# Wider output matmuls for three of four row blocks: 512 columns per row tile, and the last 128 columns transposed for 512 rows at once

## Chip, cores and metric

One core of a Trainium2 chip. The metric is the device time of one execution in microseconds (us). Every result below is the median of several executions, except where it says "one look" (a single execution), next to executions of the kernel before on the same chip.

## The reference, cut to what matters

```python
xn = layernorm(x)                                   # x: 2048 rows x 640
q  = xn @ wq                                        # 32 heads of 192
s  = softmax(q @ k.T * 192**-0.5) @ v @ wo          # the last 512 keys of the cache
g  = silu((silu(xn @ w_gate) * (xn @ w_up)) @ w_down)
out = x + s * g                                     # 2048 x 640, bf16
```

The kernel works on 4 blocks of 512 rows (0 to 3) and on 16 pairs of heads. "Block pass" is one block for one pair of heads.

## The kernel before

After the feed-forward part come 16 pairs. For each pair: query and score matmuls of four blocks, then the attention-times-V matmuls of four blocks, woven with the output matmuls (`wo`) of the block pass two back. Nearly all of this runs on half of the array's rows: `lo` is rows 0 to 63, `hi` is rows 64 to 127. The two halves work on different products at the same time and write to different PSUM banks. PSUM is the memory that TensorE adds its products up in; VectorE or ScalarE has to read a PSUM tile out before the program may use it again.

```python
def ffn_down(b, u):                     # 8 units a block, 12 matmuls of 320 columns each
    ti, n = divmod(u, 2)
    ...
    for f in range(NF):
        nc.tensor.matmul(dn[:, 0:HD], hTs[b][:, f, ti * P : (ti + 1) * P], wd_sb[:, f, cols], ...)
    nc.scalar.activation(g2[:, t, cols], dn[:, 0:HD], ACT.Silu)

def wo_turn(st, i, qt, turn):           # a row tile: 2 x 320 columns; the halves change banks between turns
    for j in range(3):
        for k, r in enumerate((lo, hi)):
            n = k ^ turn
            m = nc.tensor.matmul(ps[:, n, 0:HD], OTs[i][r, 3 * qt + j, :], wo[r, j, n * HD : (n + 1) * HD], ...)
            after(m, st)                # turn 1 waits for a small GpSimd memset that follows turn 0
    ...

def woven(i):                           # a, b: the two halves of attention; w, x, y, z: four row tiles
    (a, b), (w, x, y, z) = (pv(i, 0), pv(i, 1)), (wo_tile(i - 2, qt) for qt in range(4))
    for part in (*a[:2], drop, w[0], *b[:2], w[1], x[0], *a[2:], x[1], y[0], *b[2:], y[1], z[0]):
        part()
    held.append(z[1])                   # runs where the next pass says drop
```

`x[0]` and `x[1]` are the two turns of one unit. A unit holds one of two `sc` PSUM tiles until VectorE has added it to the sum in SBUF. `a` and `b` hold one of two `mm` tiles each until VectorE has made reciprocals and ScalarE has copied the quotients out.

The softmax here doesn't subtract the row's maximum and nothing guards it: scores larger than these inputs give would overflow.

Of the kernel before, what the change touches and what calls it, by code (L numbers as in the profile page):

```python
# [15 lines left out]
def kernel(  # L16
# [34 lines left out]
    HD = D // 2  # L51
    scale = float(Dh) ** -0.5
# [29 lines left out]
    g2 = res.tile([P, T, D], bf, name="g2")  # L82
# [83 lines left out]
    with ExitStack() as fctx:  # L166
# [125 lines left out]

        def ffn_down(b, u):
            ti, n = divmod(u, 2)
            t = b * 4 + ti
            cols = slice(n * HD, (n + 1) * HD)
            dn = mm_tile()[:, 0, :]
            for f in range(NF):
                nc.tensor.matmul(  # L299
                    dn[:, 0:HD], hTs[b][:, f, ti * P : (ti + 1) * P], wd_sb[:, f, cols],  # L300
                    start=(f == 0), stop=(f == NF - 1),
                )
            nc.scalar.activation(g2[:, t, cols], dn[:, 0:HD], ACT.Silu)

# [66 lines left out]
        for b in range(NB):  # L371
# [4 lines left out]
            for f in range(NF):  # L376
# [9 lines left out]
                if nx and f in (6, 7):  # L386
                    for t in range(4 * b + 2 * f - 8, 4 * b + 2 * f - 6):
                        ln_apply(t)
                        ln_transpose_dma(t)

                if b >= 1 and f % 3:
                    ffn_down(b - 1, u)
                    u += 1
# [27 lines left out]
    sacc = sapool.tile([P, T, D], f32, name="sacc")  # L421
# [4 lines left out]
    Ps, OTs, Obs, xrs = {}, {}, {}, {}  # L426
# [111 lines left out]
    def load_xr(t):  # L538
        xrs[t] = finp.tile([P, D], bf, name="x_r", bufs=8)
        nc.sync.dma_start(out=xrs[t][:], in_=x2[t * P : (t + 1) * P, :])  # L540


# [9 lines left out]

    HALVES = [slice(n * HD, (n + 1) * HD) for n in range(2)]

# [16 lines left out]
    def wo_turn(st, i, qt, turn):  # L571
        ps = st["sc"]
        for j in range(3):
            for k, r in enumerate((lo, hi)):
                n = k ^ turn
                m = nc.tensor.matmul(  # L576
                    ps[:, n, 0:HD], OTs[i][r, 3 * qt + j, :], pairs[i // NB]["wo"][r, j, n * HD : (n + 1) * HD],
                    start=(turn == 0 and j == 0), stop=(turn == 1 and j == 2), skip_group_check=True,
                )
                after(m, st)  # L580
# [3 lines left out]
    def wo_tile(i, qt):  # L584

        pr, b = divmod(i, NB)
        t = 4 * b + qt
        st = {}

        def first():  # L590
            st["sc"] = sc_tile()
            wo_turn(st, i, qt, 0)

        def second():
            sc = st["sc"]
            wo_turn(st, i, qt, 1)
            s_t = sacc[:, t, :].rearrange("p (n d) -> p n d", n=2)
            if pr == 0:
                nc.vector.tensor_copy(out=s_t, in_=sc[:, :, 0:HD])
            else:  # L600
                nc.vector.tensor_tensor(s_t, s_t, sc[:, :, 0:HD], ALU.add)  # L601
            if pr == last - 1 or late(i + NB):
                nc.gpsimd.tensor_tensor(sacc[:, t, :], sacc[:, t, :], g2[:, t, :], ALU.mult)
                if pr < last - 1:
                    add_x(t)

        return [first, second]

    def wo_full(i, qt):
        pr, b = divmod(i, NB)  # L610
        t = 4 * b + qt
        sc = sc_tile()
        for n in range(2):
            wo_cols(sc[:, n, 0:HD], i, qt, HALVES[n])
        s_t = sacc[:, t, :].rearrange("p (n d) -> p n d", n=2)
        if pr == 0:
            nc.vector.tensor_copy(out=s_t, in_=sc[:, :, 0:HD])
        else:
            nc.vector.tensor_tensor(s_t, s_t, sc[:, :, 0:HD], ALU.add)

        if pr == last - 1 or late(i + NB):
            nc.gpsimd.tensor_tensor(sacc[:, t, :], sacc[:, t, :], g2[:, t, :], ALU.mult)
            if pr < last - 1:
                add_x(t)

    def add_x(t):
        nc.gpsimd.tensor_tensor(sacc[:, t, :], sacc[:, t, :], xrs[t][:], ALU.add)
# [3 lines left out]
    def finish(ps, t, cols, ob, s_f, eng):  # L631

        like = (lambda a: a.rearrange("p (n d) -> p n d", n=2)) if len(ps.shape) == 3 else (lambda a: a)
        to = ps if eng is V else like(s_f[:, cols])
        V.tensor_tensor(to, ps, like(g2[:, t, cols]), ALU.mult)
        eng.tensor_tensor(like(ob[:, cols]), to, like(sacc[:, t, cols]), ALU.add)  # L636

    def wo_last(b, qt, eng):
        i, t = last * NB + b, 4 * b + qt
        ob = xrs[t] if b < 2 else finp.tile([P, D], bf, name="ob", bufs=6)  # L640
        s_f = finp.tile([P, D], f32, name="s_f", bufs=4)
        sc = mm_tile() if b == 2 and qt % 2 == 0 else sc_tile()
        for n, cols in enumerate(HALVES):
            if late(i):
                wo_cols(sc[:, n, 0:HD], i - NB, qt, cols, end=False)
            wo_cols(sc[:, n, 0:HD], i, qt, cols, first=not late(i))
        finish(sc[:, :, 0:HD], t, slice(0, D), ob, s_f, eng)
        stores.append((t, ob))

    def wo_parts(qt, parts):  # L650
# [3 lines left out]
        ob = finp.tile([P, D], bf, name="ob", bufs=6)  # L654
        s_f = finp.tile([P, D], f32, name="s_f", bufs=4)
        for n, (width, eng, queue) in enumerate(parts):
# [4 lines left out]
            finish(ps, t, cols, ob, s_f, eng)  # L661
# [4 lines left out]

# [116 lines left out]
```

## Time and profile before

| | before |
|---|---|
| median of 4 runs | 922.73 us |
| span of the profiled run | 920.7 us |
| TensorE busy, share of the span | 914.6 us, 99% |
| start to the first 512-column matmul of the feed-forward part | 14.5 us |
| feed-forward part, to the first half-row query matmul | 152.6 us |
| pairs and tail, to the last matmul | 749.6 us |
| last matmul to the end | 4.0 us |

The last four rows cut the span at the starts of three matmuls. The lines that carry the bound are in the prediction. The Trainium skill ("Trainium Kernel Development and Optimization", "Performance Expectations") warns that matmul busy time is a bad metric for the distance to the roofline, because matmuls are pipelined.

### The profile page before, as it was taken

What the parts mean: (1) busy time and instruction counts of PE and PEld (TensorE: products, weight loads), DVE (VectorE), ACT (ScalarE), POOL (GpSimd) and SP (SyncE); (2) the same over time, 40 slices, a digit from 0 to 9 for tenths busy, and PEclk for the clock granted to TensorE, in tenths of its full rate; (3) what the DMA queues carried; (4) which work ended last, traced back from release to release, by engine and by line L of the source; (5) the groups of instructions that cost most, each with busy time, mean ns of one, the idle gap of its engine ahead of it and who ended that gap; (6) DMA issues with size and microseconds to landing.
All of it is one profiled execution on the core that took longest, in us unless ns stands there. A gap on an engine that the chain in (4) does not pass through costs nothing.

```text
span 920.7 us, 25767 instructions
## 1 busy us (share of the span) xinstructions
PE 914.6 (99%) x11086; PEld 625.9 (68%) x11102; DVE 575.8 (63%) x847; ACT 474.6 (52%) x850; POOL 101.9 (11%) x390
## 2 busy tenths in 40 slices
PE   9999999999999999999999999999999999999998
PEld 5455556575858585868686767676777777676666
DVE  6343331467676767676766667676767676767656
ACT  4222222556464646565556565655555555556461
POOL 0000000000000000000000000000000000002978
PEclk9999999999999999999999999999999999999999
DMA  9330510045644444435536262635271717163524
GB/s 308 64 75 18 110 35 1 1 78 89 92 74 85 82 83 83 79 87 70 97 62 104 60 108 53 113 48 119 44 122 36 130 37 126 31 129 86 130 62 142
DMA packets 243762, 77.18 MB, mean 84 GB/s; under 512 B 224576, under 2 KB 243648, under 8 KB 243648
## 3 DMA queue, kind: packets, MB, share of 16 engines
q1 hardware_dynamic: 243216, 75.14, 41.9%
q8 instruction: 87, 1.43, 0.7%
q10 hardware_dynamic: 432, 0.39, 0.2%
q14 instruction: 27, 0.22, 0.1%
HBM read 39.45 MB, written 2.62 MB: 46 GB/s over the span
## 4 chain that ended last, share of the span: by engine, by line
PE 98%; POOL 0%; DMA 0%; DVE 0%; issue 0%; POOLq 0%; ACT 0%; DVEq 0%
PE mm L440 22%; PE sc L576 19%; PE sc L454 18%; PE mm L479 16%; PE sc L277 11%; PE mm L299 6%; PE sc L548 2%; PE mm L531 2%; POOL ob L636 0%; PE gu L277 0%; PE mm L548 0%; PE mm L312 0%; DMA x_t<-in_A_x_dram 0%; PE sc L479 0%; PE sc L531 0%
## 5 line engine op out<-in xcount | busy, mean ns | idle before, releaser
L458 ACT ACTIVATE p_t<-sc 128x1024 bf16<-128x1024 f32 x254 | 253.0, 1023 | 128.2 <-PE sc L454 128.2
L445 DVE TENSOR_REDUCE qT<-mm 128x512 bf16<-128x1024 f32 x189 | 231.1, 1223 | 95.3 <-PE mm L440 92.8
L509 ACT ACTIVATE O_b<-mm,r 128x192 bf16<-128x192 f32 x486 | 165.0, 422 | 180.8 <-issue 156.3
L440 PE MATMUL mm<-xnT,wq_p 64*128 64x512 bf16 x1890 | 240.2, 376 | 0.0
L601 DVE TENSOR_TENSOR sacc<-sacc,sc 128x640 f32<-128x640 f32 x200 | 164.2, 821 | 87.0 <-PE sc L576 87.0
L576 PE MATMUL sc<-wo_p,OT_b 64*128 64x320 bf16 x2592 | 217.3, 296 | 0.0
L454 PE MATMUL sc<-qT,khat 64*128 64x512 bf16 x1524 | 198.2, 376 | 0.0
L479 PE MATMUL mm<-V_p,p_t 64*128 64x193 bf16 x3520 | 186.4, 242 | 0.0
L479 PEld LDWEIGHTS <-p_t 64*128 64x128 bf16 x3584 | 162.9, 93 | 12.1
L440 PEld LDWEIGHTS <-wq_p 64*128 64x128 bf16 x1890 | 105.7, 94 | 93.4 <-issue 0.5
L576 PEld LDWEIGHTS <-OT_b 64*128 64x128 bf16 x2592 | 140.4, 94 | 21.4
L454 PEld LDWEIGHTS <-khat 64*128 64x128 bf16 x1536 | 85.9, 94 | 79.8
L564 POOL MEMSET turn_t<- 128x1 f32 x328 | 32.5, 99 | 691.9 <-PE mm L479 469.7
L285 DVE TENSOR_TENSOR hT<-sc,sg 128x512 bf16<-128x512 f32 x46 | 31.7, 691 | 83.7 <-ACT sg L284 83.7
L284 ACT ACTIVATE sg<-sc 128x512 bf16<-128x512 f32 x46 | 27.3, 597 | 73.4 <-PE sc L277 71.9
L277 PE MATMUL sc<-xnT,wg_sb 128*128 128x512 bf16 (+1 forms) x248 | 59.5, 353 | 0.7
L277 PE MATMUL sc<-xnT,wu_sb 128*128 128x512 bf16 (+1 forms) x259 | 60.2, 354 | 0.1
L299 PE MATMUL mm<-wd_sb,hT 128*128 128x320 bf16 x384 | 56.6, 299 | 0.0
L498 DVE RECIPROCAL r<-mm 128x4 f32<-128x4 f32 x124 | 22.6, 182 | 46.9 <-PE mm L479 36.1
L299 PEld LDWEIGHTS <-hT 128*128 128x128 bf16 x384 | 37.6, 98 | 18.9
L277 PEld LDWEIGHTS <-wu_sb 128*128 128x128 bf16 x285 | 27.1, 98 | 26.9 <-issue 0.2
L277 PEld LDWEIGHTS <-wg_sb 128*128 128x128 bf16 x285 | 27.1, 98 | 22.7
(69 smaller groups left out, 374.9 us busy)
## 6 DMA issues: line engine op xcount, KB each, us to landing
wo_p<-in_A_wo_dram SPq DMA_DIRECT2D x16, 480.0 KB, 4.4
K_p<-in_A_k_cache_dram SPq DMA_DIRECT2D x32, 192.0 KB, 3.3
V_p<-in_A_v_cache_dram SPq DMA_DIRECT2D x32, 192.0 KB, 3.0
wq_p<-in_A_wq_dram SPq DMA_DIRECT2D x64, 80.0 KB, 3.0
wq_p<-in_A_wq_dram SPq DMA_DIRECT2D x16, 160.0 KB, 3.4
x_r<-in_A_x_dram SPq DMA_DIRECT2D x16, 160.0 KB, 4.7
x_t<-in_A_x_dram SPq DMA_DIRECT2D x14, 160.0 KB, 3.0
OT_b<-O_b SPq DMA_TRANSPOSE x124, 3.0
```

What stands on the lines that cost most here:

```text
L277: nc.tensor.matmul(out, w_sb[:, c, f * P : (f + 1) * P], xnT[:, c, qc], start=(c == 0), stop=(c == NC - 1),)
L285: nc.vector.tensor_tensor(hTs[b][:, f, :], u, sg[:], ALU.mult)
L299: nc.tensor.matmul(dn[:, 0:HD], hTs[b][:, f, ti * P : (ti + 1) * P], wd_sb[:, f, cols], start=(f == 0), stop=(f == NF - 1),)
L440: nc.tensor.matmul(q_ps[:, h, :], pairs[pr]["wq"][r, c, j * P : (j + 1) * P], xnT[r, c, b * 512 : (b + 1) * 512], start=(c == 0), stop=(c ...
L445: nc.vector.reduce_sum(qTs[i][:, j, :], q_ps[:, :, :].rearrange("p h n -> p n h"), axis=AX.X)
L454: nc.tensor.matmul(sc[:, h, :], khat[r, j, ks], qT[r, j, :], start=(j == 0), stop=(j == 2))
L458: nc.scalar.activation(p_t[:, :, :], sc[:, :, :], ACT.Exp, scale=scale)
L479: m = nc.tensor.matmul(acc[:, k, h * 256 : h * 256 + Dh + 1], Ps[i][kc][r, h, qt * P : (qt + 1) * P], V_p[r, kc, h, 0 : Dh + 1], start=(p ...
L509: nc.scalar.activation(O_b[:, qt, h, :], a_k[:, h, 0:Dh], ACT.Copy, scale=r[:, k, h, :])
L564: st["turn"] = nc.gpsimd.memset(turn_t[:], 0.0)
L576: m = nc.tensor.matmul(ps[:, n, 0:HD], OTs[i][r, 3 * qt + j, :], pairs[i // NB]["wo"][r, j, n * HD : (n + 1) * HD], start=(turn == 0 and j ...
L601: nc.vector.tensor_tensor(s_t, s_t, sc[:, :, 0:HD], ALU.add)
```

## The change

Intent: matmuls of 512 columns instead of 320. 640 columns do not divide by 512. So blocks 0 to 2 take columns 0 to 511 by row tile, and the last 128 columns the other way round: the 128 columns of the weight are the stationary operand and 512 rows stream. I call this unit the remainder. That part of the sum is transposed in memory, so x is brought in transposed for it, and a DMA transposes the result back at the end. Block 3, which is finished last, keeps the old form. The core of the diff:

```diff
+        def x_transpose(t):
+            nc.sync.dma_start_transpose(out=xT[:, t // 4, ...], in_=x_t[t][:, MC:D])
...
                     for t in range(4 * b + 2 * f - 8, 4 * b + 2 * f - 6):
                         ln_apply(t)
                         ln_transpose_dma(t)
+                        if t < 4 * MB:
+                            x_transpose(t)
+                if b == 0 and f in (8, 9):
+                    for t in (2 * f - 16, 2 * f - 15):
+                        x_transpose(t)
-                if b >= 1 and f % 3:
+                if b >= 1 and f in (1, 3, 5, 7, 9):
                     ffn_down(b - 1, u)          # 4 units of 512 columns and one of 512 rows
...
+        def rest():                             # the remainder: last 128 columns, 512 rows
+            sc = sc_tile()
+            for n, r in enumerate((lo, hi)):
+                wo_rest(sc[:, n, :], i, r)      # three matmuls of 512 for lo, then three for hi
+            for n in range(2):
+                add_sum(pr + n, s_t[:, b, :], sc[:, n, :])
+        if b == MB:
+            return [unit([(qt, cols) for cols in HALVES]) for qt in range(4)]
+        return [unit([(2 * h + k, MAIN) for k in range(2)]) for h in range(2)] + [rest]
...
+        else:                                   # blocks 0 to 2: two units of two row tiles, and the remainder
+            w, x, left = units
+            order = (*a[:2], drop, *b[:2], w[0], *a[2:], x[0], w[1], *b[2:], x[1])
...
+        if q2:                                  # tail
+            store_block(b)                      # 512 rows x 640 columns in one store
+    last_rest(2, V, sc_tile)                    # ends with the DMA transpose of o_t
```

(Cut: sums and products renamed to `s_m`, `s_t`, `s_o`, `g_m`, `g_t`, `g_o`; the full-row versions for the last two pairs; the gates on GpSimd.)

More of the change, by code (lines that the diff above doesn't have):

```diff
@@ L51 @@
     HD = D // 2
+    MB = NB - 1
+    MC = D - P
     scale = float(Dh) ** -0.5
@@ L81 @@
     xnT = res.tile([P, NC, Sq], bf, name="xnT")
-    g2 = res.tile([P, T, D], bf, name="g2")
+    g_m = res.tile([P, 4 * MB, MC], bf, name="g_m")
+    g_t = res.tile([P, MB, 512], bf, name="g_t")
+    g_o = res.tile([P, 4, D], bf, name="g_o")
+    xT = res.tile([P, MB, 512], bf, name="xT")
     ident = consts.tile([P, P], bf, name="ident")
@@ L291, in ffn_hidden @@
             hidden_gate(b, f, *gu)
+        def x_transpose(t):
+            nc.sync.dma_start_transpose(
+                out=xT[:, t // 4, (t % 4) * P : (t % 4 + 1) * P], in_=x_t[t][:, MC:D]
+            )
         def ffn_down(b, u):
-            ti, n = divmod(u, 2)
-            t = b * 4 + ti
-            cols = slice(n * HD, (n + 1) * HD)
             dn = mm_tile()[:, 0, :]
-            for f in range(NF):
-                nc.tensor.matmul(
-                    dn[:, 0:HD], hTs[b][:, f, ti * P : (ti + 1) * P], wd_sb[:, f, cols],
-                    start=(f == 0), stop=(f == NF - 1),
-                )
-            nc.scalar.activation(g2[:, t, cols], dn[:, 0:HD], ACT.Silu)
+            if b == MB:
+                ti, n = divmod(u, 2)
+                cols = slice(n * HD, (n + 1) * HD)
+                dn, to = dn[:, 0:HD], g_o[:, ti, cols]
+            elif u < 4:
+                ti, cols = u, slice(0, MC)
+                to = g_m[:, 4 * b + u, :]
+            else:
+                to = g_t[:, b, :]
+            for f in range(NF):
+                if b < MB and u == 4:
+                    at, by = wd_sb[:, f, MC:D], hTs[b][:, f, :]
+                else:
+                    at, by = hTs[b][:, f, ti * P : (ti + 1) * P], wd_sb[:, f, cols]
+                nc.tensor.matmul(dn, at, by, start=(f == 0), stop=(f == NF - 1))
+            nc.scalar.activation(to, dn, ACT.Silu)
         def q_full(i, j):
@@ L420 @@
     finp = ctx.enter_context(tc.tile_pool(name="fin", bufs=2))
-    sacc = sapool.tile([P, T, D], f32, name="sacc")
+    s_m = sapool.tile([P, 4 * MB, MC], f32, name="s_m")
+    s_t = sapool.tile([P, MB, 512], f32, name="s_t")
+    s_o = sapool.tile([P, 4, D], f32, name="s_o")
     NS = NPAIR * NB
@@ L425 @@
     last = NPAIR - 1
-    Ps, OTs, Obs, xrs = {}, {}, {}, {}
+    Ps, OTs, Obs, xbs = {}, {}, {}, {}
     def q_rows(i, j, between=None):
@@ L536, in pv_full, with load_xb, rows @@
         divide(i, q2, acc, alone and (0,))
-    def load_xr(t):
-        xrs[t] = finp.tile([P, D], bf, name="x_r", bufs=8)
-        nc.sync.dma_start(out=xrs[t][:], in_=x2[t * P : (t + 1) * P, :])
+    def load_xb(b):
+        xbs[b] = finp.tile([P, 4, D], bf, name="x_b", bufs=NB)
+        n = MC if b < MB else D
+        nc.sync.dma_start(
+            out=xbs[b][:, :, 0:n],
+            in_=x2[b * 512 : (b + 1) * 512, 0:n].rearrange("(t p) d -> p t d", p=P),
+        )
+    def rows(b, qts):
+        if b == MB:
+            return s_o[:, qts, :], g_o[:, qts, :]
+        t = slice(4 * b + qts.start, 4 * b + qts.stop)
+        return s_m[:, t, :], g_m[:, t, :]
     def late(i):
@@ L551, in wo_cols, with wo_rest @@
             )
+    def wo_rest(ps, i, r=slice(0, P), first=True, end=True):
+        for j in range(3):
+            nc.tensor.matmul(
+                ps.rearrange("p (t q) -> p t q", q=P), pairs[i // NB]["wo"][r, j, MC:D],
+                OTs[i][:, :, :].rearrange("p (t j) q -> p j t q", j=3)[r, j, :, :],
+                start=(first and j == 0), stop=(end and j == 2),
+            )
     HALVES = [slice(n * HD, (n + 1) * HD) for n in range(2)]
+    MAIN = slice(0, MC)
     def follows(m, earlier):
@@ L569, in after, with wo_turn @@
             follows(m, st.pop("turn"))
-    def wo_turn(st, i, qt, turn):
+    def wo_turn(st, i, tiles, turn):
         ps = st["sc"]
         for j in range(3):
-            for k, r in enumerate((lo, hi)):
-                n = k ^ turn
+            for n, r in enumerate((lo, hi)):
+                k = n ^ turn
+                qt, cols = tiles[k]
                 m = nc.tensor.matmul(
-                    ps[:, n, 0:HD], OTs[i][r, 3 * qt + j, :], pairs[i // NB]["wo"][r, j, n * HD : (n + 1) * HD],
+                    ps[:, k, 0 : cols.stop - cols.start], OTs[i][r, 3 * qt + j, :],
+                    pairs[i // NB]["wo"][r, j, cols],
                     start=(turn == 0 and j == 0), stop=(turn == 1 and j == 2), skip_group_check=True,
@@ L582, in wo_turn @@
             turned(m, st)
-    def wo_tile(i, qt):
-        pr, b = divmod(i, NB)
-        t = 4 * b + qt
-        st = {}
-        def first():
-            st["sc"] = sc_tile()
-            wo_turn(st, i, qt, 0)
-        def second():
-            sc = st["sc"]
-            wo_turn(st, i, qt, 1)
-            s_t = sacc[:, t, :].rearrange("p (n d) -> p n d", n=2)
-            if pr == 0:
-                nc.vector.tensor_copy(out=s_t, in_=sc[:, :, 0:HD])
-            else:
-                nc.vector.tensor_tensor(s_t, s_t, sc[:, :, 0:HD], ALU.add)
-            if pr == last - 1 or late(i + NB):
-                nc.gpsimd.tensor_tensor(sacc[:, t, :], sacc[:, t, :], g2[:, t, :], ALU.mult)
-                if pr < last - 1:
-                    add_x(t)
-        return [first, second]
@@ L609, in wo_full @@
-    def wo_full(i, qt):
-        pr, b = divmod(i, NB)
-        t = 4 * b + qt
-        sc = sc_tile()
-        for n in range(2):
-            wo_cols(sc[:, n, 0:HD], i, qt, HALVES[n])
-        s_t = sacc[:, t, :].rearrange("p (n d) -> p n d", n=2)
-        if pr == 0:
-            nc.vector.tensor_copy(out=s_t, in_=sc[:, :, 0:HD])
-        else:
-            nc.vector.tensor_tensor(s_t, s_t, sc[:, :, 0:HD], ALU.add)
-        if pr == last - 1 or late(i + NB):
-            nc.gpsimd.tensor_tensor(sacc[:, t, :], sacc[:, t, :], g2[:, t, :], ALU.mult)
-            if pr < last - 1:
-                add_x(t)
@@ L626, in add_x, with add_sum @@
-    def add_x(t):
-        nc.gpsimd.tensor_tensor(sacc[:, t, :], sacc[:, t, :], xrs[t][:], ALU.add)
-    stores = []
-    def finish(ps, t, cols, ob, s_f, eng):
-        like = (lambda a: a.rearrange("p (n d) -> p n d", n=2)) if len(ps.shape) == 3 else (lambda a: a)
-        to = ps if eng is V else like(s_f[:, cols])
-        V.tensor_tensor(to, ps, like(g2[:, t, cols]), ALU.mult)
-        eng.tensor_tensor(like(ob[:, cols]), to, like(sacc[:, t, cols]), ALU.add)
-    def wo_last(b, qt, eng):
-        i, t = last * NB + b, 4 * b + qt
-        ob = xrs[t] if b < 2 else finp.tile([P, D], bf, name="ob", bufs=6)
-        s_f = finp.tile([P, D], f32, name="s_f", bufs=4)
-        sc = mm_tile() if b == 2 and qt % 2 == 0 else sc_tile()
-        for n, cols in enumerate(HALVES):
-            if late(i):
-                wo_cols(sc[:, n, 0:HD], i - NB, qt, cols, end=False)
-            wo_cols(sc[:, n, 0:HD], i, qt, cols, first=not late(i))
-        finish(sc[:, :, 0:HD], t, slice(0, D), ob, s_f, eng)
-        stores.append((t, ob))
+    def add_sum(pr, to, ps):
+        if pr == 0:
+            nc.vector.tensor_copy(out=to, in_=ps)
+        else:
+            nc.vector.tensor_tensor(to, to, ps, ALU.add)
@@ new lines, in sum_rows, with gate @@
+    def sum_rows(i, qts, sc):
+        pr, b = divmod(i, NB)
+        to, g = rows(b, qts)
+        if b == MB:
+            to = to.rearrange("p t (n d) -> p (t n) d", n=2)
+            sc = sc[:, :, 0:HD]
+        add_sum(pr, to, sc)
+    def gate(i, qts=None):
+        pr, b = divmod(i, NB)
+        if not (pr == last - 1 or late(i + NB)):
+            return
+        to, g = (s_t[:, b, :], g_t[:, b, :]) if qts is None else rows(b, qts)
+        nc.gpsimd.tensor_tensor(to, to, g, ALU.mult)
+        if pr < last - 1:
+            add_x(b, qts)
@@ new lines, in add_x, with wo_units, unit, first @@
+    def add_x(b, qts=None):
+        if qts is None:
+            to, x = s_t[:, b, :], xT[:, b, :]
+        else:
+            to, x = rows(b, qts)[0], xbs[b][:, qts, 0 : MC if b < MB else D]
+        nc.gpsimd.tensor_tensor(to, to, x, ALU.add)
+    def wo_units(i):
+        pr, b = divmod(i, NB)
+        def unit(tiles):
+            st, qts = {}, slice(tiles[0][0], tiles[1][0] + 1)
+            def first():
+                st["sc"] = sc_tile()
+                wo_turn(st, i, tiles, 0)
+            def second():
+                wo_turn(st, i, tiles, 1)
+                sum_rows(i, qts, st["sc"][:, :, :])
+            return [first, second]
+        def rest():
+            sc = sc_tile()
+            for n, r in enumerate((lo, hi)):
+                wo_rest(sc[:, n, :], i, r)
+            for n in range(2):
+                add_sum(pr + n, s_t[:, b, :], sc[:, n, :])
+        if b == MB:
+            return [unit([(qt, cols) for cols in HALVES]) for qt in range(4)]
+        return [unit([(2 * h + k, MAIN) for k in range(2)]) for h in range(2)] + [rest]
@@ new lines, in wo_full @@
+    def wo_full(i, q2):
+        pr, b = divmod(i, NB)
+        if b == MB:
+            units = [[(qt, cols) for cols in HALVES] for qt in (2 * q2, 2 * q2 + 1)]
+        else:
+            units = [[(2 * q2 + k, MAIN) for k in range(2)]]
+        for tiles in units:
+            sc, qts = sc_tile(), slice(tiles[0][0], tiles[1][0] + 1)
+            for k, (qt, cols) in enumerate(tiles):
+                wo_cols(sc[:, k, 0 : cols.stop - cols.start], i, qt, cols)
+            sum_rows(i, qts, sc[:, :, :])
+            gate(i, qts)
+        if b < MB and q2:
+            sc = sc_tile()
+            wo_rest(sc[:, 0, :], i)
+            add_sum(pr, s_t[:, b, :], sc[:, 0, :])
+            gate(i)
@@ new lines, with finish, last_rows @@
+    stores = []
+    def finish(ps, to, s, g, eng):
+        s_f = ps
+        if eng is not V:
+            s_f = finp.tile([P, 2, MC], f32, name="s_f", bufs=3)
+            if len(ps.shape) == 2:
+                s_f = s_f[:, :, :].rearrange("p n d -> p (n d)")[:, 0 : ps.shape[1]]
+            else:
+                s_f = s_f[:, 0 : ps.shape[1], :]
+        V.tensor_tensor(s_f, ps, g, ALU.mult)
+        eng.tensor_tensor(to, s_f, s, ALU.add)
+    def last_rows(b, qts, eng, tile_of):
+        i = last * NB + b
+        ps = tile_of()
+        for k, qt in enumerate(range(qts.start, qts.stop)):
+            if late(i):
+                wo_cols(ps[:, k, :], i - NB, qt, MAIN, end=False)
+            wo_cols(ps[:, k, :], i, qt, MAIN, first=not late(i))
+        finish(ps[:, 0 : qts.stop - qts.start, :], xbs[b][:, qts, 0:MC], *rows(b, qts), eng)
@@ L650, in wo_parts, with last_rest @@
+    def last_rest(b, eng, tile_of):
+        i = last * NB + b
+        ps = tile_of()[:, 0, :]
+        if late(i):
+            wo_rest(ps, i - NB, end=False)
+        wo_rest(ps, i, first=not late(i))
+        o_t = finp.tile([P, 512], bf, name="o_t", bufs=2)
+        finish(ps, o_t[:], s_t[:, b, :], g_t[:, b, :], eng)
+        nc.sync.dma_start_transpose(out=xbs[b][:, :, MC:D], in_=o_t[:])
     def wo_parts(qt, parts):
         i, t, c0 = NS - 1, 4 * (NB - 1) + qt, 0
-        ob = finp.tile([P, D], bf, name="ob", bufs=6)
@@ L655, in wo_parts @@
-        s_f = finp.tile([P, D], f32, name="s_f", bufs=4)
+        ob = xbs[MB][:, qt, :]
         for n, (width, eng, queue) in enumerate(parts):
@@ L660, in wo_parts @@
             wo_cols(ps, i, qt, cols, first=False)
-            finish(ps, t, cols, ob, s_f, eng)
+            finish(ps, ob[:, cols], s_o[:, qt, cols], g_o[:, qt, cols], eng)
             if queue:
@@ L665, in wo_parts, with store_block @@
             stores.append((t, ob))
+    def store_block(b):
+        nc.sync.dma_start(
+            out=out2[b * 512 : (b + 1) * 512, :].rearrange("(t p) d -> p t d", p=P), in_=xbs[b][:]
+        )
     def store(left):
@@ L669, in store @@
             t, ob = stores.pop(0)
-            nc.sync.dma_start(out=out2[t * P : (t + 1) * P, :], in_=ob[:])
+            nc.sync.dma_start(out=out2[t * P : (t + 1) * P, :], in_=ob)
     held = []
@@ L683, in woven @@
     def woven(i):
-        (a, b), (w, x, y, z) = (pv(i, 0), pv(i, 1)), (wo_tile(i - 2, qt) for qt in range(4))
-        for part in (*a[:2], drop, w[0], *b[:2], w[1], x[0], *a[2:], x[1], y[0], *b[2:], y[1], z[0]):
+        a, b, units = pv(i, 0), pv(i, 1), wo_units(i - 2)
+        if (i - 2) % NB == MB:
+            w, x, y, z = units
+            order = (*a[:2], drop, w[0], *b[:2], w[1], x[0], *a[2:], x[1], y[0], *b[2:], y[1], z[0])
+            left = z[1]
+        else:
+            w, x, left = units
+            order = (*a[:2], drop, *b[:2], w[0], *a[2:], x[0], w[1], *b[2:], x[1])
+        for part in order:
             part()
-        held.append(z[1])
+        held.append(left)
     for pr in range(NPAIR):
@@ L709 @@
                 if pr >= last - 1:
-                    for t in range(8):
-                        load_xr(t + 8 if pr < last else t)
+                    for n in range(2):
+                        load_xb(n + 2 if pr < last else n)
                         if pr == last:
-                            add_x(t)
+                            for qt in range(4):
+                                add_x(n, slice(qt, qt + 1))
+                            add_x(n)
         if pr == last:
@@ L726 @@
                     pv_full(i, q2)
-                    wo_full(i - 2, 2 * q2)
-                    wo_full(i - 2, 2 * q2 + 1)
+                    wo_full(i - 2, q2)
             if b == 0 and pr + 2 < NPAIR:
@@ L740 @@
     for b, q2, more in ((0, 0, (2, 1)), (0, 1, (3, 0)), (1, 0, (3, 1)), (1, 1, None)):
-        for k in range(2):
-            wo_last(b, 2 * q2 + k, G)
+        last_rows(b, slice(2 * q2, 2 * q2 + 2), G, sc_tile)
+        if q2:
+            last_rest(b, V if b else G, mm_tile if b else sc_tile)
         if more:
             pv_full(i + more[0], more[1])
-    for qt in range(4):
-        store(3)
-        wo_last(2, qt, G if qt else V)
+        if q2:
+            store_block(b)
+    last_rest(2, V, sc_tile)
+    last_rows(2, slice(0, 2), G, mm_tile)
+    last_rows(2, slice(2, 3), V, sc_tile)
+    last_rows(2, slice(3, 4), G, mm_tile)
     for qt, engs in enumerate(((G, V), (G, G), (V, G))):
-        store(2 - qt)
+        if qt == 1:
+            store_block(2)
+        elif qt:
+            store(0)
         wo_parts(qt, [(HD, eng, None) for eng in engs])
```

## The prediction

> **What bounds the kernel now.** I read the busy shares first, then the chain that ended last, then the groups, and then the timeline of single stretches, because only there can the rate of one matmul be seen.
>
> ```profile
> PE 914.6 (99%) x11086; PEld 625.9 (68%) x11102; DVE 575.8 (63%) x847; ACT 474.6 (52%) x850; POOL 101.9 (11%) x390
> PE 98%; POOL 0%; DMA 0%; DVE 0%; issue 0%; POOLq 0%; ACT 0%; DVEq 0%
> L440 PE MATMUL mm<-xnT,wq_p 64*128 64x512 bf16 x1890 | 240.2, 376 | 0.0
> L601 DVE TENSOR_TENSOR sacc<-sacc,sc 128x640 f32<-128x640 f32 x200 | 164.2, 821 | 87.0 <-PE sc L576 87.0
> L576 PE MATMUL sc<-wo_p,OT_b 64*128 64x320 bf16 x2592 | 217.3, 296 | 0.0
> ```
>
> TensorE is busy 99% and is 98% of the chain; it idles 0.0 us before the output matmuls (L576). VectorE has 37% of the span free. So the time moves with two things: what TensorE's instruction stream costs when it never waits, and whether the change makes it wait. The timeline of one stretch gives the first:
>
> ```profile
> 560.23 0.85 PE L479 MATMUL mm<-V_p,p_t 64*128 64x193 bf16 x16
> 560.89 0.59 PE L576 MATMUL sc<-wo_p,OT_b 64*128 64x320 bf16 x6
> 561.30 0.85 PE L479 MATMUL mm<-V_p,p_t 64*128 64x193 bf16 x16
> ...
> 583.54 0.83 PE L440 MATMUL mm<-xnT,wq_p 64*128 64x512 bf16 x6
> 584.19 0.59 PE L576 MATMUL sc<-wo_p,OT_b 64*128 64x320 bf16 x6
> 584.59 0.61 PE L440 MATMUL mm<-xnT,wq_p 64*128 64x512 bf16 x4
> ```
>
> Start to start: 16 matmuls of 193 columns take 0.66 us, 6 of 320 take 0.41 us, 6 of 512 take 0.65 us. Each matmul uses 64 rows of the array, and the program alternates the lower 64 rows (lo) with the upper 64 (hi), so these are 8, 3 and 3 pairs: 83, 136 and 216 ns a pair. That is 2.4 columns a nanosecond plus some 2.6 ns. A pair costs its columns and almost nothing else: a weight load for every matmul and the bank changes are already hidden.
>
> **What the Trainium skill says.** "TensorE: Matmul & The Clock Gate", section "Wait — 56ns, not 53.3ns?", gives N / 2.4 GHz plus about 2.5 ns for back-to-back warm matmuls. The trace agrees (216 ns at 512, 136 at 320). So fewer, longer matmuls save only about 2.6 ns each. The same page, "Part 3: Packing small matmuls", says that matmuls on different row groups overlap, but that matmuls start and end in program order, without reordering. The trace agrees as far as it can: 6 matmuls of 64 rows take 3 slots of 216 ns, because the next matmul is always for the other half. "TensorEngine Tiling (Array Packing)", "Gotcha 1: PSUM Pressure", says that two row tiles may not use one PSUM bank at once; that is why the code gives lo and hi different banks. No page that I found gives the issue cost of a DMA transpose; I take it from the trace.
>
> **The change, part by part.**
>
> A. Fewer instructions. From the built programs: matmuls on full rows go from 1500 to 1329, on half rows from 9602 to 8864, with exactly the same columns (510464 and 3275264). At 2.6 ns for each full matmul and each pair: (171 + 738 / 2) x 2.6 ns = **-1.4 us**. This is all that TensorE can gain. The intent is sound, the overhead it attacks is just small.
>
> B. The order of the new remainder. The last 128 columns of a block become one unit of 3 lo and 3 hi matmuls of 512 columns (lo sums to one bank, hi to the other, no bank change). In the built program they stand as lo, lo, lo, hi, hi, hi; every other half-row matmul of both programs alternates. A lo after a lo must wait 216 ns for its own half, and the hi behind it can't pass. With starts at 0, 216, 432 (lo), 452, 668, 884 (hi), the hi half is free at 1100 ns instead of 668. If 193- or 320-column pairs follow, both halves wait for that: 432 ns lost. If 512-column pairs follow, lo runs ahead by one matmul and the loss is 256 ns at first, but the rest is lost when the phase ends. So 432 ns each. There are 41 such units (54 block passes in the half-row scheme, less 13 of block 3): 41 x 0.432 = **+17.7 us**. This lies wholly on TensorE, the path that sets the end.
>
> C. New waits for PSUM in the woven phase. Before, each unit was evacuated by one VectorE add of 640 columns (821 ns). Now a pair of row tiles takes an add of 1024 columns, estimated at 1.22 us (the 1024-column reduction takes 1223 ns), and the remainder takes two adds of 512, one after the other, some 0.69 us each (a 512-column product out of PSUM takes 691 ns). Both wait for the last hi matmul, and they start 0.21 us after it (562.38 to 562.59 in the timelines). The remainder's tile is thus free about 0.21 + 0.69 + 0.06 + 0.69 + 0.06 = 1.7 us after its stream ends. When block 3's units follow, in the old order, the second of them needs that tile 0.41 (first half unit) + 0.66 (attention) + 0.41 = 1.48 us later: 0.2 to 0.25 us of wait, 13 times, 3 us. Where the remainder falls between query matmuls, the two adds push back the query reduction, and the third query group waits about 0.1 us, 14 times. For the accumulators the balance is even: the longer add delays the reciprocals by 0.5 us, but the slow remainder gives that time back. I take **+4 us**, and 1 to 6 as likely; these are differences of small numbers.
>
> D. VectorE itself: per block pass 4 x 0.82 = 3.3 us become 2 x 1.22 + 2 x 0.69 = 3.8 us, 41 times +0.5 = 22 us more, on an engine with 340 us idle. It costs only what C says. GpSimd does the same elements in other portions.
>
> E. The transposes of x in the first block. A DMA transpose holds the issuing queue about 1.2 us however small it is (the group of xnT has a median of 1224 ns at 640 columns).
>
> ```profile
> 25.46 5.89 SPq L268 DMA_TRANSPOSE xnT<-xn  x4
> 31.40 2.00 SPq L183 DMA_DIRECT2D x_t<-in_A_x_dram  x4
> ...
> 33.90 1.24 PE L277 MATMUL sc<-xnT,wg_sb 128*128 128x512 bf16 x5
> ```
>
> The four take 5.9 us, the fourth lands 2.6 us after its issue, at about 32.7, and block 1 begins at 33.90: 1.2 us of slack. In the changed program the queue's order is xnT, x, xnT, x, xnT, x, xnT, so three more stand before the fourth: its issue moves from 30.1 to about 33.4, its landing to 36. TensorE waits **+2.1 us**, once. In block 1 the same pattern has over 5 us to spare because the down matmuls lie between.
>
> F. The tail. Adding up the last 30 us in the new order, TensorE, VectorE and GpSimd meet at the same points. The queue has three transposes more and three large stores in place of twelve small ones; the last large store should go out near 914 and land by 919, as the final small store does. **+0.3 us**.
>
> Sum: 922.9 - 1.4 + 17.7 + 4 + 2.1 + 0.3 = 945.6. I say **945 us**.
>
> **Rivals.** First: the order of the remainder costs nothing, because the array starts a hi matmul as soon as its half is free, or queues both halves apart. Then B is zero; C shrinks or grows (the remainder's 0.43 us of slack is gone, so waits for accumulators of up to 0.3 us would appear), and the time is 922 to 929. For it speaks only that no trace here has two neighbours on the same rows; against it the skill's statement on order. I give it 7%. Second: VectorE's longer adds become the bound of the woven phase. A woven pass would have 3.8 + 0.4 us of VectorE in about 6.3 us, so there is room, and its idle time before the adds (87 us) says the same; only the order of releases in C can hurt, at worst 6 to 8 us, giving 949. Third: the saved instructions matter more than I think, since the matmul group counts 296 ns each for 133 ns of columns. But the timeline shows that those 296 overlap; a gain beyond 2 us would contradict it. Fourth: C and E are hidden anyway, and only A and B remain: 939, just inside 2%.
>
> **Range and chances.** The firm part is A + B: 939.2. C, E and F add 1 to 9, almost certainly nothing below zero, so 8 in 10 lies between 939.5 and 949. The border of 2% is 941.3. With C + E + F under 2.1 (about one in ten) or the first rival (7%) it stays within 2%; so slower 0.82, same 0.17, faster 0.01.
>
> **What would show each step.** B: in the timeline of the woven phase the remainder's 6 matmuls take about 1.08 us start to start instead of 0.65, 41 times. A: two row tiles take 0.65 us each turn, 216 ns a pair. C: idle time of TensorE before block 3's output matmuls, ended by VectorE, some 0.2 us each, and adds near 1.22 and 0.69 us. E: a gap of about 2 us on TensorE near 34 us, ended by a DMA. F: TensorE's last matmul to the end unchanged at about 3.8 us. The prediction is wrong if the remainder takes 0.65 us; then little is left of the slowdown.

## The result, and the profile after

936.54 us (median of 4 runs, 935.69 to 937.35) against 922.73 us. A ratio here is the mean time of one kernel's fast runs over that of the other's in the same rounds, so not quite the ratio of the medians: 1.015, with a 95% interval of 1.0135 to 1.0165. It is slower, by less than 2%. The predicted 945 us was too high, and the time lies outside the stated range (939.5 to 949).

| | before | changed |
|---|---|---|
| span of the profiled run | 920.7 us | 933.8 us |
| start to first 512-column matmul | 14.5 us | 15.1 us |
| feed-forward part | 152.6 us | 155.0 us |
| pairs and tail, to the last matmul | 749.6 us | 757.6 us |
| last matmul to the end | 4.0 us | 6.1 us |

The first row of the stages is noise: over all profiled runs below, of both kernels and all variants, it lies between 14.4 and 15.6 us. So the change cost 2.4 + 8.0 + 2.1 us in three places. The page of the changed kernel, whole lines:

```profile
PE 920.3 (99%) x10193; PEld 557.6 (60%) x10193; DVE 593.0 (63%) x844; ACT 473.2 (51%) x841; POOL 91.0 (10%) x302
L504 PE MATMUL mm<-V_p,p_t 64*128 64x193 bf16 x3520 | 183.1, 242 | 2.8 <-ACT O_b L534 2.8
L624 PE MATMUL sc<-wo_p,OT_b 64*128 64x512 bf16 (+1 forms) x1608 | 181.7, 345 | 0.0
L637 DVE TENSOR_TENSOR s_m<-s_m,sc 128x1024 f32<-128x1024 f32 x82 | 100.1, 1221 | 46.0 <-PE sc L624 39.7
L282 PE MATMUL sc<-xnT,wg_sb 128*128 128x512 bf16 (+1 forms) x260 | 60.2, 354 | 2.5 <-DMA xnT<-xn 2.4
L637 DVE TENSOR_TENSOR s_t<-s_t,sc 128x512 f32<-128x512 f32 x82 | 56.3, 687 | 5.0
```

The adds have the predicted lengths (1221 and 687 ns). TensorE now has idle time, but little: 2.8 us before attention, ended by ScalarE, and 2.4 us, ended by the transposes of xn.

The first view to read is TensorE's timeline in the woven phase of one pair (columns: start us, duration us, engine, line, operation, count, and in brackets the idle time and what ended it). L592 is the remainder.

```profile
574.39 0.83 PE L592 MATMUL sc<-OT_b,wo_p 64*128 64x512 bf16 x6
575.21 0.58 PE L624 MATMUL sc<-wo_p,OT_b 64*128 64x320 bf16 x6
...
586.45 0.82 PE L592 MATMUL sc<-OT_b,wo_p 64*128 64x512 bf16 x6
587.44 0.84 PE L504 MATMUL mm<-V_p,p_t 64*128 64x193 bf16 x16 [0.16 <-ACT O_b L534]
...
592.67 0.83 PE L592 MATMUL sc<-OT_b,wo_p 64*128 64x512 bf16 x6
593.32 0.61 PE L465 MATMUL mm<-xnT,wq_p 64*128 64x512 bf16 x4
```

Three remainders in one pair. The third, among query matmuls, takes 593.32 - 592.67 = 0.65 us start to start. That is 3 x 216 ns: the same as three alternating pairs, although the program has lo, lo, lo, hi, hi, hi. The predicted 1.08 us is not there. The first and second take 0.82 and 0.99 us, 0.17 and 0.34 too long. Only 0.16 us of this shows as idle time: a matmul counts as busy until its modelled end, some 0.16 us after it has streamed (375 ns for 213 ns of columns), so a wait of 0.17 us leaves no trace in the idle column. VectorE and ScalarE name the causes:

```profile
573.94 1.22 DVE L637 TENSOR_TENSOR s_m<-s_m,sc 128x1024 f32<-128x1024 f32 x1
...
584.68 1.22 DVE L637 TENSOR_TENSOR s_m<-s_m,sc 128x1024 f32<-128x1024 f32 x1 [1.04 <-PE sc L624]
585.82 0.18 DVE L523 RECIPROCAL r<-mm 128x4 f32<-128x4 f32 x1
```

```profile
586.03 1.36 ACT L534 ACTIVATE O_b<-mm,r 128x192 bf16<-128x192 f32 x4 [0.95 <-DVE r L523]
```

The add of the second unit ends at 573.94 + 1.22 = 575.16, and block 3's first unit, which needs that tile, starts at 575.21. In the other place the reciprocal of the second accumulator stands behind the 1024-column add and starts right at its end. Its attention matmuls had been streamed by 585.13, and the usual distance in the kernel before is 0.29 us, so it is 0.4 us late. ScalarE's four copies end at 587.39, and attention, which needs the accumulator, starts at 587.44.

The start of block 1 in the feed-forward part; the issuing queue, then TensorE:

```profile
26.11 1.32 SPq L273 DMA_TRANSPOSE xnT<-xn  x1
27.47 1.23 SPq L299 DMA_TRANSPOSE xT<-x_t  x1
...
34.52 1.22 SPq L273 DMA_TRANSPOSE xnT<-xn  x1
```

```profile
33.47 1.24 PE L282 MATMUL sc<-xnT,wu_sb 128*128 128x512 bf16 x5
37.12 1.25 PE L282 MATMUL sc<-xnT,wg_sb 128*128 128x512 bf16 x5 [2.42 <-DMA xnT<-xn]
```

The queue is held 1.23 us even by a transpose of 128 x 128. The fourth transpose of xn is issued at 34.52, and TensorE starts block 1 2.6 us later, at 37.12. This is step E as predicted (2.1 us): 2.42 us in the idle column, and 2.6 us by the starts (37.12 - 33.47, less the 1.08 us that five such matmuls take).

And the issuing queue in the tail:

```profile
918.80 1.31 SPq L743 DMA_TRANSPOSE x_b<-o_t  x1
921.55 0.38 SPq L762 DMA_DIRECT2D out_dram<-x_b  x1
922.02 1.80 SPq L743 DMA_TRANSPOSE x_b<-o_t  x1
927.39 0.37 SPq L762 DMA_DIRECT2D out_dram<-x_b  x1
927.85 2.28 SPq L769 DMA_DIRECT2D out_dram<-x_b  x3
930.22 0.52 SPq L757 DMA_DIRECT2D out_dram<-x_b  x1
```

The store of block 2 (927.39) must wait for the transpose that was issued at 922.02. It lands only 5.3 us after issue (2.4 us is the fastest of the three), since it stands behind block 1's store of 640 KB. Four small stores, which would have gone out earlier, queue up behind it. The last one is issued at 930.22, 2.7 us after the last group of three matmuls begins (927.54). In the kernel before it was 1.6 us (918.04 after 916.45).

### The profile page after: what moved, and what is told of

It reads as the page before. It is cut to its first block, busy times and chain, and to the rows that moved or that the text cites. A ratio compares the mean times of both kernels' runs of the same rounds, so it can differ in the third digit from the quotient of the medians.

```text
span 933.8 us, 23745 instructions
## 1 busy us (share of the span) xinstructions
PE 920.3 (99%) x10193; PEld 557.6 (60%) x10193; DVE 593.0 (63%) x844; ACT 473.2 (51%) x841; POOL 91.0 (10%) x302
## 5 line engine op out<-in xcount | busy, mean ns | idle before, releaser
L504 PE MATMUL mm<-V_p,p_t 64*128 64x193 bf16 x3520 | 183.1, 242 | 2.8 <-ACT O_b L534 2.8
L504 PEld LDWEIGHTS <-p_t 64*128 64x128 bf16 x3584 | 159.7, 93 | 39.3 <-issue 7.4
L624 PE MATMUL sc<-wo_p,OT_b 64*128 64x512 bf16 (+1 forms) x1608 | 181.7, 345 | 0.0
L637 DVE TENSOR_TENSOR s_m<-s_m,sc 128x1024 f32<-128x1024 f32 x82 | 100.1, 1221 | 46.0 <-PE sc L624 39.7
L624 PEld LDWEIGHTS <-OT_b 64*128 64x128 bf16 x1608 | 80.7, 93 | 38.8 <-issue 3.9
L610 POOL MEMSET turn_t<- 128x1 f32 x246 | 24.3, 99 | 705.7 <-PE mm L504 571.8
L637 DVE TENSOR_TENSOR s_t<-s_t,sc 128x512 f32<-128x512 f32 x82 | 56.3, 687 | 5.0
L637 DVE TENSOR_TENSOR s_o<-s_o,sc 128x640 f32<-128x640 f32 x52 | 42.7, 821 | 15.1 <-PE sc L624 14.3
L321 PE MATMUL mm<-wd_sb,hT 128*128 128x512 bf16 (+1 forms) x240 | 46.8, 347 | 0.0
```

The lines of the kernel that those rows point to most:

```text
L321: nc.tensor.matmul(dn, at, by, start=(f == 0), stop=(f == NF - 1))
L504: m = nc.tensor.matmul(acc[:, k, h * 256 : h * 256 + Dh + 1], Ps[i][kc][r, h, qt * P : (qt + 1) * P], V_p[r, kc, h, 0 : Dh + 1], start=(p ...
L624: m = nc.tensor.matmul(ps[:, k, 0 : cols.stop - cols.start], OTs[i][r, 3 * qt + j, :], pairs[i // NB]["wo"][r, j, cols], start=(turn == 0 ...
L637: nc.vector.tensor_tensor(to, to, ps, ALU.add)
```

## The experiments

Twelve runs were made (the last is the changed kernel once more), all with a correct result by the comparison with the reference. The kernel before took 922.5 to 922.7 us beside each group.

### The order of the remainder

```diff
-            for n, r in enumerate((lo, hi)):
-                wo_rest(sc[:, n, :], i, r)
+            for j in range(3):
+                for n, r in enumerate((lo, hi)):
+                    nc.tensor.matmul(sc[:, n, :], wo[r, j, MC:D], OTs[i][r, ...], start=(j == 0), stop=(j == 2))
```

> The changed kernel with the six matmuls of the remainder in the order lo, hi, lo, hi, lo, hi instead of three lo and three hi. Theory of the prediction (a lo after a lo waits and the hi behind it cannot pass, 41 x 0.432 us): about 17 us less than the changed kernel, so 919 to 921 us. Rival (the order costs nothing): 936 us, and the remainder still takes 0.65 us start to start in the timeline, as it already does in the changed kernel.

935.7 us (4 runs, 934.82 to 936.72); the changed kernel itself gave 936.5 and, in a later group, 935.4. The order costs nothing. Step B of the prediction, 17.7 us, falls.

The question is then how. For this the hi matmuls of the remainder were cut to 384 columns, so that the trace can tell them from the lo ones (the sum of the last 128 rows is left incomplete; the tolerance of the comparison did not notice):

```diff
             for n, r in enumerate((lo, hi)):
+                tn = 4 - n                      # lo: 4 x 128 columns, hi: 3 x 128
                 for j in range(3):
-                    matmul(sc[:, n, :], ..., OTs[i][r, j, all four tiles])
+                    matmul(sc[:, n, 0 : tn * P], ..., OTs[i][r, j, 0:tn])
```

> Wrong result on purpose: the changed kernel with the three hi matmuls of the remainder cut to 384 columns, so that lo (512) and hi (384) can be told apart in the trace; program order stays lo, lo, lo, hi, hi, hi. If the array keeps program order, the trace shows three 512s 216 ns apart and then three 384s. If the halves are queued apart, 512s and 384s alternate, some 20 ns apart, and each half runs at its own pace.

936.04 us in one look. Groups by form in the first 0.21 us of one remainder (column four is the form, then the count):

```profile
L687 PE MATMUL sc<-OT_b,wo_p 64*128 64x384 bf16 x2 | 0.5, 322 | 0.0
...
L687 PE MATMUL sc<-OT_b,wo_p 64*128 64x512 bf16 x1 | 0.4, 376 | 0.0
```

The window runs from 593.39 to 593.60. One lo (512) and already two hi (384) overlap it. The single records start at 593.393 (512), 593.413 (384), 593.576 (384), 593.609 (512), 593.738 (384), 593.825 (512). So the lo's start 216 ns apart, the hi's 163 ns apart, each at its own pace, and every hi starts ahead of a lo that stands before it in the program. The program that was built has lo, lo, lo, hi, hi, hi. Whether the reordering is done in the array or between the built program and the array these records alone don't say; the next runs speak for a queue of limited length.

```diff
 # kernel before, scores: 256 groups of three lo, then three hi
-        for j in range(3):
-            for h, r in enumerate((lo, hi)):
+        for h, r in enumerate((lo, hi)):
+            for j in range(3):
 # in other runs: attention in runs of four (kc inside r) or of eight (kc and head inside r);
 # query in runs of five (c inside r)
```

> The kernel before with every group of score matmuls (256 groups) in the order three lo, three hi. Program order kept by the array: at least 256 x 0.256 = 65 us and at most 110 us more, 988 to 1033 us. Halves queued apart: no change, 922 to 924 us.

923.21 us, one look, 0.5 us above the kernel before. Free.

> The kernel before with the attention matmuls in runs of four lo, four hi of 193 columns (448 runs). Within the same limit: no change, 922 to 924 us. If short matmuls leave the array no time to look ahead, a part of 448 x 3 x 83 ns = 112 us.

923.68 us, one look, 1.2 us above. Free, or nearly so: its start took 15.6 us instead of 14.5, and its three other stages agree with those of the kernel before within 0.1 us.

> The kernel before with the attention matmuls of each half turn in runs of eight lo, then eight hi (224 such runs of 193 columns). Program order kept: 7 slots x 83 ns x 224 = 130 us more, about 1050 us. Halves queued apart without limit: no change. A limited window: something between, and the timeline shows how many of a run go ahead.

940.38 us, one look: 17.7 us more for 224 runs, 79 ns each. That is one slot of 83 ns per run and not the seven that strict order would cost. The single records of the trace show where it goes. A slot is the time of one matmul on its half. In one run the eight lo start at 570.520, 570.603, 570.689, 570.771, 570.854, 570.936, 571.023 and 571.105. The hi half has streamed its last score matmul by 570.72, but the first hi starts only at 570.862, 8 ns after the fifth lo. The same, 8 or 9 ns after the fifth lo and with three lo still to come, stands in 217 places of this trace. So hi does not go ahead while four lo matmuls wait in front of it, and does with three. Runs of three and of four leave two and three waiting as soon as the first lo has started, and they are free.

> The kernel before with every query group (189) in the order five lo, five hi of 512 columns. From the run with eights, where the first hi begins with the third lo, so that five lo wait ahead of it: a run of five is within that, so no change, 922 to 924 us. If the limit lies at four, each group loses a slot of 216 ns: 41 us more.

932.65 us, one look: 10.1 us more, which neither side had expected. The timeline shows that most of it comes from my edit and not from the fives:

```profile
588.55 1.02 PE L576 MATMUL sc<-wo_p,OT_b 64*128 64x320 bf16 x12
589.85 0.58 PE L576 MATMUL sc<-wo_p,OT_b 64*128 64x320 bf16 x6 [0.28 <-POOL turn_t L564]
590.27 1.26 PE L440 MATMUL mm<-xnT,wq_p 64*128 64x512 bf16 x9
591.35 0.38 PE L454 MATMUL sc<-qT,khat 64*128 64x512 bf16 x1
```

With the loops exchanged, the held half unit stood right after its first half and had to wait for the bank change (0.44 to 0.49 us start to start), and the first group of each phase lost one more slot of 0.21 us. That slot is the same limit: in the group at 590.267 the second lo starts at 590.483 and the first hi at 590.491, again with three lo waiting and not with four. (The expectation had five as the limit, since it counted the run of eight from its third lo. Its other branch, a slot lost in each of 189 groups, did not come either: the hi half runs one slot behind for the whole phase, and the slot is lost once.) The two together, some 14 times, are 9 to 10 us. After that the groups of five run at 1.08 us each (590.27 to 591.35), which is 5 x 216 ns: free in the steady state. A clean run of fives was not made.

### The transposes of x

```diff
-                        if t < 4 * MB:
+                        if b and t < 4 * MB:
                             x_transpose(t)
-                if b == 0 and f in (8, 9):
+                if b == 0 and f >= 8:
```

> The changed kernel with the transposes of x of block 0 issued after those of the normalized rows, no longer between them. Theory (three transposes ahead of the fourth make TensorE wait once at the start of block 1): the gap of 2.4 us near 37 us goes, 934 us against 936.5 of the changed kernel. Rival (the wait is only moved, the later loads of x then hold up block 2): 936 us, with a new gap later.

932.40 us (4 runs, 932.26 to 932.55), ratio to before 1.0106 (1.0091 to 1.0121). The gap is gone:

```profile
25.47 5.80 SPq L273 DMA_TRANSPOSE xnT<-xn  x4
31.32 10.15 SPq L299 DMA_TRANSPOSE xT<-x_t  x8
```

```profile
32.83 1.24 PE L282 MATMUL sc<-xnT,wu_sb 128*128 128x512 bf16 x5
33.91 1.24 PE L282 MATMUL sc<-xnT,wg_sb 128*128 128x512 bf16 x5
```

The feed-forward part takes 152.4 us, 0.2 us less than before the change, and no new wait follows. Step E is shown. (The medians differ by 3 to 4 us, the stage by 2.6; runs of the changed kernel alone scatter over 1.7 us.)

### The order of the halves of the units

```diff
-            order = (*a[:2], drop, *b[:2], w[0], *a[2:], x[0], w[1], *b[2:], x[1])
+            order = (*a[:2], drop, *b[:2], w[0], *a[2:], w[1], x[0], *b[2:], x[1])
```

> The changed kernel with the second half of the first unit moved ahead of the first half of the second (w1 before x0) in the woven phase, so that the 1024-column add is over before the second reciprocal is due. Theory (the add stands before the reciprocal on VectorE, the accumulator is freed late, attention waits 0.34 us): the wait after the remainder falls from 0.34 to about 0.05 us, 14 times, so about 4 us less than the changed kernel, 932 to 933 us. The wait of 0.17 us before block 3's first output matmuls, which hangs on the second unit's add, stays. Rival (the wait is for ScalarE's four copies themselves): no change, 936 us.

930.73 us (4 runs, 930.44 to 932.47), ratio 1.0092 (1.0077 to 1.0107). Pairs and tail fall from 757.6 to 752.9 us. VectorE and TensorE at the place that was shown above:

```profile
583.20 0.83 PE L592 MATMUL sc<-OT_b,wo_p 64*128 64x512 bf16 x6
583.85 0.85 PE L504 MATMUL mm<-V_p,p_t 64*128 64x193 bf16 x16
```

```profile
580.79 1.22 DVE L637 TENSOR_TENSOR s_m<-s_m,sc 128x1024 f32<-128x1024 f32 x1 [0.40 <-PE sc L624]
582.17 0.18 DVE L523 RECIPROCAL r<-mm 128x4 f32<-128x4 f32 x1 [0.16 <-PE mm L504]
```

The reciprocal now waits for TensorE and not for the add, and the remainder takes 583.85 - 583.20 = 0.65 us before attention too. So the wait of 0.34 us was made by the place of the add on VectorE, and the edit takes all of it away, 14 times.

### The stores of the tail

```diff
-        if q2:
+        if q2 and b == 0:
             store_block(b)
     last_rest(2, V, sc_tile)
+    store_block(1)
```

> The changed kernel with the store of block 1 issued after the transpose back of block 2, not before it. Theory (that transpose waits behind a store of 640 KB and lands 5.3 us after its issue, which holds back block 2's store and the last small stores behind it): the time from the last matmul to the end falls from 6.3 to 4.3 to 4.8 us, 1.5 to 2 us less, 934.5 us. Rival (the end hangs on the bytes still to be written): less than 0.5 us.

934.25 us (4 runs, 933.26 to 936.15), ratio 1.0129 (1.0113 to 1.0144). From the last matmul to the end it takes 4.4 us instead of 6.1:

```profile
918.00 2.67 SPq L743 DMA_TRANSPOSE x_b<-o_t  x2
920.78 2.68 SPq L762 DMA_DIRECT2D out_dram<-x_b  x2
923.91 3.72 SPq L769 DMA_DIRECT2D out_dram<-x_b  x3
928.36 0.33 SPq L757 DMA_DIRECT2D out_dram<-x_b  x1
```

No transpose takes more than 2.6 us to land, and no store piles up. The interval of this run's ratio overlaps that of the changed kernel; the stage is what shows it.

### All three, and a version without the remaining waits

> The three edits together. If the three causes are apart: 2.4 + 4 + 1.7 = about 8 us less than the changed kernel, 928 to 929 us, still 5 to 6 us above the kernel before, of which 2.7 us are the waits before block 3's output matmuls and some 1.3 us waits of the first pair. If they hide one another, less.

926.07 us (4 runs, 925.88 to 927.05), ratio 1.0041 (1.0024 to 1.0058). The gains add up: the three stages show 2.6 + 5.1 + 1.5 = 9.2 us against the changed kernel, where about 8 was expected.

The last version takes away the wait of block 3's first unit, too, by another order, and moves the first unit of pair 0:

```diff
         if (i - 2) % NB == MB:
-            order = (*a[:2], drop, w[0], *b[:2], w[1], x[0], *a[2:], x[1], y[0], *b[2:], y[1], z[0])
-            left = z[1]
+            order = (*a[:2], drop, *b[:2], w[0], *a[2:], w[1], x[0], *b[2:], x[1], y[0])
+            left = [[y[1], z[0]], [z[1]]]       # two groups, dropped at two places of the next pass
         else:
+            order = (*a[:2], drop, *b[:2], drop, w[0], *a[2:], w[1], x[0], *b[2:], x[1])
+            if i == 2:
+                order = (*a[:2], w[0], *b[:2], *a[2:], w[1], x[0], *b[2:], x[1])
```

> The three edits together and, besides, block 3's units woven in the new order (the first of them after the second accumulator's attention, its last half units held over to the next pass), and the first pass of pair 0 with its first unit ahead of the second accumulator. Theory (block 3's first unit waits 0.17 us for the second unit's add, 13 times, and a few waits of 0.03 us behind it; pair 0 waits 0.4 us): 2.7 + 0.4 us less than the three edits alone, 922.9 us, so even with the kernel before, with 1.4 us of fewer instructions against 0.6 us in pair 0 and 0.6 us at the end. Rival (the waits only move to the next unit): 926 us.

922.75 us (5 runs, 922.63 to 922.95) against 922.52 us; ratio 1.0001 (0.9989 to 1.0014). Pairs and tail take 749.15 us, 0.4 us less than in the kernel before, with one wait of 0.6 us left in pair 0 (the scores wait for the two adds of a remainder). The end takes 4.55 us instead of 4.0. So it is even with the kernel before, not better.

> The changed kernel once more, on the chip of these runs, as a yardstick: 935.5 to 937.5 us, 1.3 to 1.6% above the kernel before.

935.36 us (4 runs, 934.82 to 936.51), ratio 1.0141 (1.0126 to 1.0157). Its stages: 155.1, 757.5 and 6.2 us, as in the first profile within 0.2 us.

## Why the prediction was wrong

**The bound and A.** Right. The columns are the cost. With the waits gone, pairs and tail are 0.4 us shorter with a wait of 0.6 us in them, which makes 1.0 us for A's share there (369 pairs and 63 full matmuls, 1.1 us predicted). The feed-forward part gained 0.2 us (0.3 predicted).

**B, the failed step.** In the prediction's words: "A lo after a lo must wait 216 ns for its own half, and the hi behind it can't pass." It can. The remainder takes 0.65 us with three lo in front, the alternating order changes nothing, and the marked run shows hi matmuls starting ahead of earlier lo ones. 17.7 us became 0. The sign that the prediction named for this, "The prediction is wrong if the remainder takes 0.65 us", came true; that "little is left of the slowdown" did not, since 13.8 us are left. The error was to carry a statement of the skill ("MATMULs are pc-monotone in start AND end — strict FIFO, no reordering") to a case that no trace had shown, and to give the rival that it doesn't hold 7%. The prediction had itself noted that the trace agrees only "as far as it can".

**C, right kind of wait, wrong places.** 4 us predicted. From the starts: 0.34 us before attention 14 times (4.8 us), 0.17 us before block 3's first unit and 0.03 us behind it 13 times (2.7 us), 0.36 us once more before attention, and 1.1 us in pair 0. That is 8.9 us; less A's 1.1 it agrees with the measured 8.0. The prediction put the wait at block 3's second unit (0.2 to 0.25 us; the 0.03 us above is this wait) and at the third query group (0.1 us; the starts show 0.01), and called the accumulators even. By its own sums this follows from B: it had the remainder 0.43 us too long, which covers a wait of 0.34 us before attention and one of 0.17 us before block 3's first unit. Its first rival said exactly this ("waits for accumulators of up to 0.3 us would appear"), but estimated the sum too low, at 922 to 929 us, since block 3's unit, pair 0 and the tail were not in it.

**D.** Right: VectorE's busy time rises by 17 us (22 predicted) without being a bound; its order matters, not its load.

**E.** Right, 2.6 us for 2.1 (the stage shows 2.4, since A's 0.2 us goes off).

**F.** Wrong in size: 2.1 us for 0.3. The prediction had the last large store going out near 914, as on the old clock of the tail, i.e. some 2.7 us before the last matmul starts; it went out with the last matmuls. Its sum gives no time to a transpose that lands behind a large store: this one took 5.3 us, where the fastest took 2.4.

**Sum.** 922.7 - 1.4 + 0 + 8.9 + 2.6 + 2.1 = 934.9 us, and some noise of the start, against 935.4 to 936.5 measured; the rest is within the scatter of single runs. C, E and F were too small by some 7 us together, which hid that much of the 17.7 us that B had too much: that the number was off by 9 us and not by more is luck. What stays open: what holds hi back when four lo wait (matmuls or weight loads that are queued), and whether that is so in other programs; runs of five to eight were tried in two forms, one look each.

## What to carry to other kernels

Before you merge matmuls, divide what one instruction costs beyond its columns: here 2.6 ns, so 28% fewer output matmuls were worth about 1 us. Wider units lengthen the evacuation behind them; look on the evacuating engine for what stands in the queue behind a longer add, and order the work so that a short, urgent instruction doesn't follow a long one. On a saturated engine, compare starts with starts: here a wait of 0.17 us, with modelled ends some 0.16 us late, did not show as idle time.

## What the Trainium skill lacked or had wrong

- "TensorE: Matmul & The Clock Gate", "Part 3: Packing small matmuls — row/col tiling", has strict program order for matmuls. The runs show that matmuls of the two 64-row halves pass each other: 384-column hi matmuls at 593.413, 593.576 and 593.738 between lo ones at 593.393, 593.609 and 593.825, with a program order of lo, lo, lo, hi, hi, hi. Runs of three (923.2 us) and of four (923.7 us) cost nothing but noise of the start against 922.7 and 922.5; runs of eight cost 79 ns each (940.4 us). In the runs of five and of eight, hi went ahead with three lo waiting and not with four. That the program as built was not reordered on its way to the array is not shown.
- The page "DMA: Bandwidth & Descriptors", section "DMA Transpose (X-bar)", has no time for which a transpose holds the issuing queue; the page's only counts for that stand in a table about another generation's fast path, and none is for a small transpose from SBUF to SBUF. Here it is about 1.2 us for 128 x 128 as for 128 x 640.
- No page that I found tells what a transpose's landing costs behind a large store on the same queue: 5.3 us instead of 2.4 us behind 640 KB.
- "Trainium Kernel Development and Optimization", "Performance Expectations", is right that matmul busy time misleads. It could add the size: here a lost 0.34 us showed as 0.16 us of idle time, and 0.17 us as none.
